# Attention and mixture of experts on one core: x of three batches written in rows of 2 KB, w2 loaded in runs of eight rows

## The chip, the cores and the metric

The kernel runs on one core of a Trainium2 chip. The metric is the device time of one execution in microseconds (us). A profile gives the span of one execution, which is some 1.5 us shorter than the time (201.9 of 203.35 us in the profiled run of before, 207.6 of 209.21 in that of after). Engines are called PE (matrix multiplications), DVE (vectors), ACT (exponentials and other functions), POOL (GpSimd: casts, and the issues of the weight loads among others) and SP (only issues transfers). A transfer is cut into packets (47,856 in the profile of before), which 16 DMA engines move.

The run list gives each run a state. On one core, a run is put down as slow when it takes over 1.5% longer than the fastest of the same kernel. This matters below, because the kernel before turns out to have two ways of running.

## The reference

```python
# attention: 4 batches, 8 heads, 768 positions, 64 wide
scores = scale * q @ k.T                  # causal; some heads see all the past,
a = softmax(where(mask, scores, -1e9))    # the others 4 sinks and a window of 64
x = (a @ v).transpose(0, 2, 1, 3).reshape(3072, 512)
# mixture of experts: 8 experts, 512 -> 1024 -> 512
do = x @ w_skip > 0                       # tokens that are computed
e, gate = argmax / softmax of x[do] @ w_gate
out = x
out[do] = x[do] + gate * (relu(x[do] @ w1[e]) @ w2[e])
```

## The kernel before

Attention runs over 16 pairs of heads, four pairs to a batch. The loads of q, k and v and the stores of x are issued by SP. POOL casts each v to 16 bits (the tile `va`), casts the result x, and issues the loads of the expert weights at six fixed pairs. So the weights of the first experts are loaded while attention still runs.

```python
def load_weight():                        # on GpSimd; half 0 is w1, half 1 is w2
    ...
        nc.gpsimd.dma_start(              # w1: 8 KB runs
            out=wts[e, 0]..., in_=w1r[e][:, q0 * w:q1 * w])
    ...
        nc.gpsimd.dma_start(              # w2: runs of WR = 4 rows
            out=wts[e, 1].rearrange("p (t r) d -> p t (r d)", r=WR)[:, q0:q1],
            in_=w2r[e][:, q0:q1])

def load_v(i):                            # ld_pool has two buffers
    vf = ld_pool.tile([P, 2, NQB, D], FP32, tag="vf", name="vf")
    for hi, hh in enumerate(hs):
        nc.sync.dma_start(out=vf[:, hi], in_=vv[b, :, hh])

# weigh(i, hi), after the product with v:
    if not last:
        ins = nc.gpsimd.tensor_copy(x16s[i], xh[:, :, h2:h2 + 2])
        if i in (0, 5, 10, 11, 12, 13):
            with tc.issue_after(ins.ins):
                load_weight()
    if i >= NPR - 2:                      # the last batch: a store for each pair
        ...
    elif i % 2 == 1:                      # the others: a store for two pairs,
        hc = (i // 2) % 2                 # half a row of x, 1 KB
        nc.sync.dma_start(
            out=Ov[b][:, :, hc * 4 * D:(hc + 1) * 4 * D],
            in_=xh.rearrange("p n h d -> p n (h d)"))

# the main loop
    cast_v(i)
    load_qk(i + 3)
    load_v(i + 2)
```

Pairs count from 0. Pairs 14 and 15 are the last two, and batch 2 consists of pairs 8 to 11. The store of x after pair 11 is issued near 92 us, and the v of pair 15 is loaded right behind it on the same queue.

The softmax here doesn't subtract the row's maximum and nothing guards it: scores larger than these inputs give would overflow.

Of the kernel before, what the change touches and what calls it, by code (L numbers as in the profile page):

```python
# [9 lines left out]
FP32 = mybir.dt.float32  # L10
FP16 = mybir.dt.float16
I32 = mybir.dt.int32
# [28 lines left out]
MASKED = 30000.0  # L41
WR = 4

# [216 lines left out]
def kernel(  # L260
# [27 lines left out]
    ones16 = const.tile([P, P], FP16, name="ones16")  # L288
    tmpi = const.tile([P, P], I32, name="tmpi")
    iota16 = const.tile([P, P], FP16, name="iota16")  # L290
# [3 lines left out]
    lim = const.tile([P, E], FP32, name="lim")  # L294
    pidi = const.tile([P, 1], I32, name="pidi")
    val = const.tile([P, N // P, 4], FP16, name="val")
    tabl = const.tile([1, H], FP32, name="tabl")
# [66 lines left out]
    wtile(E // 2, 0, wpool)  # L364
    xgs = [const.tile([P, DM], FP32, name=f"xg{t}") for t in range(NT)]


    w1r = moe_w1.rearrange("e (p s) f -> e p (s f)", p=P)
    w2r = moe_w2.rearrange("e (t p r) d -> e p t (r d)", p=P, r=WR)

# [3 lines left out]
    def load_weight(quarters=2):  # L374

        e, half, q0 = todo[0]
        q1 = q0 + quarters
        assert q1 <= 2
        del todo[:quarters]
        if half == 0:  # L380
            w = DS * F // 2
            nc.gpsimd.dma_start(
                out=wts[e, 0].rearrange("p s f -> p (s f)")[
                    :, q0 * w:q1 * w], in_=w1r[e][:, q0 * w:q1 * w])
        else:
            nc.gpsimd.dma_start(
                out=wts[e, 1].rearrange("p (t r) d -> p t (r d)", r=WR)[
                    :, q0:q1],
                in_=w2r[e][:, q0:q1])

# [19 lines left out]
    with tc.tile_pool(name="ac", bufs=1) as ac_pool, \  # L410
         tc.tile_pool(name="ld", bufs=2) as ld_pool, \
         tc.tile_pool(name="qk_in", bufs=2) as qk_in_pool, \
         tc.tile_pool(name="qt", bufs=2) as qt_pool, \
         tc.tile_pool(name="xsb", bufs=3) as x_pool, \
         tc.tile_pool(name="st_ps", bufs=2, space=bass.MemoryType.PSUM) as st_psum, \
# [193 lines left out]
        def weigh(i, hi):  # L609
# [15 lines left out]
            for n, (qb, c, vb) in enumerate(plan):  # L625
                nc.tensor.matmul(  # L626
                    opsa[:, qb, :], ats[i][:, b0 + c:b0 + c + P], vb,
                    start=(n == 0), stop=(n == len(plan) - 1))
            if i % 2 == 0 and hi == 0:
                xhs[i // 2] = x_pool.tile([P, NQB, 4, D], FP32, tag="xh",  # L630
                                          name="xh")
# [6 lines left out]
            if last:  # L638
                nc.vector.tensor_mul(x16s[i][:, :, hi], opsa[:, :, :D],
                                     rec.to_broadcast([P, NQB, D]))  # L640
            nc.vector.tensor_mul(xhs[i // 2][:, :, 2 * (i % 2) + hi, :],  # L641
                                 opsa[:, :, :D],
                                 rec.to_broadcast([P, NQB, D]))
            if hi == 0:
                return
            xh = xhs[i // 2]
            h2 = 2 * (i % 2)
            if not last:
# [4 lines left out]
            if i >= NPR - 2:  # L653
                nc.sync.dma_start(
                    out=Ov[b][:, :, hs[0] * D:(hs[1] + 1) * D].rearrange(
                        "p n (h d) -> p n h d", h=2),
                    in_=xh[:, :, h2:h2 + 2])
            elif i % 2 == 1:
                hc = (i // 2) % 2
                nc.sync.dma_start(  # L660
                    out=Ov[b][:, :, hc * 4 * D:(hc + 1) * 4 * D],
                    in_=xh.rearrange("p n h d -> p n (h d)"))

        def gate_transpose(i):
            xtp = tr_psum.tile([P, NQB, P], FP16, tag="tps", name="xtp")
            for n in range(NQB):
                nc.tensor.matmul(xtp[:, n],
                                 x16s[i][:, n].rearrange("p h d -> p (h d)"),
                                 C.ident,
                                 is_transpose=True, start=(n == 0),  # L670
                                 stop=(n == NQB - 1))
            xTg = gat_pool.tile([P, NQB, P], FP16, tag="gxT", name="gxT",
                                bufs=5)
            if i < NPR - 1:
                nc.scalar.activation(xTg, xtp, ACT.Copy)  # L675
            else:
                half = NQB // 2
                nc.vector.tensor_copy(xTg[:, :half], xtp[:, :half])
                nc.scalar.activation(xTg[:, half:], xtp[:, half:], ACT.Copy)
            xTs[i] = xTg  # L680
            if i == NPR - 2:
                nc.gpsimd.drain()
            if i == NPR - 1:

                nc.gpsimd.tensor_copy(mark, xTg[:, 0, :1])
                load_weight()
# [226 lines left out]
    with tc.tile_pool(name="moe_w", bufs=1) as mw_pool, \  # L913
# [50 lines left out]
        def first(e):  # L964
            ht = h_pool.tile([P, FS, CAP], FP16, tag="ht", name="ht")
            for f2 in range(FS // 2):
                hps = h_psum.tile([P, 2, CAP], FP32, tag="hps", name="hps")
                for fi in range(2):
                    fs = 2 * f2 + fi
                    for s in range(DS):  # L970
                        nc.tensor.matmul(  # L971
                            hps[:, fi, :],
                            wts[e, 0][:, s].rearrange(
                                "p (t c r) -> p t r c", c=P, r=WR)[
                                    :, fs // WR, fs % WR],
                            xTs[e][:, s, :], start=(s == 0),
                            stop=(s == DS - 1))
# [3 lines left out]
        def second(e):  # L981


            parts = ([(s2, 0, FS) for s2 in range(NSM)] if e < E - 1 else
                     [(s2, h, h + WR) for h in (0, WR) for s2 in range(NSM)])
            ypss = {}
# [95 lines left out]
```

## Time and profile before

| | before |
|---|---|
| time, median of 3 | 204.0 us (203.73, 204.0, 207.48) |
| span of the profiled run | 201.9 us |
| busy share of PE, ACT, POOL | 81%, 56%, 59% |
| cast of v of pairs 13, 14, 15 begins | 93.61, 108.94, 112.36 us |
| first matmul of the experts (hps) | 133.10 us |
| last matmul of the experts (yps) ends | 192.84 us |

The prediction shows the queues, the chain and the timelines. Three more views of before are wanted for comparison. The first is the stretch between attention and experts, by engine: the start and end in us, its length, then for each engine its busy time and number of instructions, then the granted PE clock, the DMA share and GB/s.

```profile
core 0: us, PE busy (x) PEld busy (x) DVE busy (x) ACT busy (x) POOL busy (x), PEclk, DMA share, GB/s
...
108.00:133.00 25.00, 17.76 (x179) 10.33 (x179) 13.93 (x46) 3.65 (x6) 12.85 (x20) 0.80 0.82 186
```

Seven of these 25 us have no PE work, and the clock was at 0.80 on average. The second view is the group of expert matmuls with the weight loads that feed them (busy us and mean ns behind the first bar):

```profile
L971 PE MATMUL hps<-xT,w 128*128 128x256 f16 x256 | 29.2, 273 | 1.2 <-DVE xT L961 1.2
L971 PEld LDWEIGHTS <-w 128*128 128x128 f16 x256 | 27.9, 113 | 2.8 <-issue 1.5
```

The third is PE's longest gap at the end of attention (start, length; in brackets the idle time before and what ended it):

```profile
109.82 1.26 PE L626 MATMUL opsa<-va,at 128*128 128x65 f16 x21 [4.03 <-POOL va L505]
```

### The profile page before, as it was taken

How to read it: one execution, taken by the hardware profiler on the slowest of the kernel's cores; microseconds unless marked ns; L12 is line 12 of the kernel's file. 1: busy time of each engine (PE TensorE's matmuls, PEld its weight loads, DVE VectorE, ACT ScalarE, POOL GpSimd, SP SyncE). 2: the span in 40 equal slices, each digit the busy share in tenths (PEclk: the TensorE clock that was granted, in tenths of full speed). 3: DMA queues.
4: the chain of work that ended last, by engine and by line, in shares of the span. 5: the costliest groups of instructions: out<-in, count | busy, mean ns of one | idle time of the engine just before them, and what ended most of it. 6: DMA issues, size and time to landing. Idle time of an engine off the chain costs nothing.

```text
span 201.9 us, 4741 instructions
## 1 busy us (share of the span) xinstructions
PE 163.2 (81%) x1896; PEld 119.3 (59%) x1896; DVE 109.5 (54%) x254; ACT 113.0 (56%) x164; POOL 119.3 (59%) x179
## 2 busy tenths in 40 slices
PE   0487999889888898888982757978999999999920
PEld 0366666676666676666852443378678678665700
DVE  5323666636899668997650678253444534534020
ACT  5998888897688977888891420035143144130400
POOL 7585499687387693788403901687858575133311
PEclk9999999999999999999998795999999999999985
DMA  5999699999899999999999899479999999999501
GB/s 173 295 345 287 169 174 238 316 327 318 236 245 201 301 343 296 342 266 214 215 275 232 204 234 174 103 181 246 232 239 233 239 245 233 235 245 248 165 14 63
DMA packets 47856, 47.12 MB, mean 233 GB/s; under 512 B 28484, under 2 KB 43588, under 8 KB 46802
## 3 DMA queue, kind: packets, MB, share of 16 engines
q0 software_dynamic: 6976, 21.56, 50.3%
q1 hardware_dynamic: 40850, 25.17, 44.3%
q8 instruction: 17, 0.28, 0.6%
q14 instruction: 13, 0.11, 0.2%
HBM read 56.64 MB, written 10.49 MB: 333 GB/s over the span
## 4 chain that ended last, share of the span: by engine, by line
ACT 27%; DMA 26%; PE 23%; issue 8%; DVE 7%; POOL 6%; POOLq 1%; SPq 0%; ACTq 0%; DVEq 0%
ACT at L606 15%; DMA out_dram<-xg,idx_s 14%; DMA vf<-in_v_dram 10%; PE pst L578 5%; ACT xg L507 4%; PE pst L588 4%; PE hps L971 4%; ACT qT L526 4%; ACT gxT L675 3%; PE opsa L626 3%; POOL out_dram L1001 2%; PE pst L595 2%; PE yps L991 2%; POOL xg L935 2%; DMA xg<-out_dram,idx_s 1%
## 5 line engine op out<-in xcount | busy, mean ns | idle before, releaser
L606 ACT ACTIVATE at<-pst 128x1024 f16<-128x1024 f32 (+2 forms) x76 | 61.3, 836 | 17.2 <-PE pst L600 13.3
L978 ACT ACTIVATE ht<-hps 128x512 f16<-128x512 f32 x32 | 19.1, 598 | 49.4 <-PE hps L971 49.4
L588 PE MATMUL pst<-qT,kz 128*128 128x128 f16 (+2 forms) x288 | 35.8, 242 | 2.5 <-ACT qT L526 2.1
L588 PEld LDWEIGHTS <-kz 128*128 128x128 f16 x288 | 24.1, 100 | 21.9 <-issue 12.8
L535 DVE COPY kz<-tps 64x768 f16<-64x768 f16 x28 | 26.6, 950 | 9.7 <-PE tps L518 9.3
L971 PE MATMUL hps<-xT,w 128*128 128x256 f16 x256 | 29.2, 273 | 1.2 <-DVE xT L961 1.2
L971 PEld LDWEIGHTS <-w 128*128 128x128 f16 x256 | 27.9, 113 | 2.8 <-issue 1.5
L578 PE MATMUL pst<-smask,ident 128*128 128x512 f16 (+1 forms) x60 | 22.3, 372 | 8.7 <-ACT at L606 8.7
L991 PE MATMUL yps<-w,ht 128*128 128x512 f16 x128 | 28.8, 379 | 0.0
L1001 POOL DMA_INDIRECT out_dram<-xg,idx_s x16 | 16.4, 1022 | 18.5 <-issue 8.5
L649 POOL CAST gx<-xh 128x768 f16<-128x768 f32 x15 | 12.4, 828 | 19.3 <-DVE xh L641 14.5
L999 DVE SCALAR_TENSOR_TENSOR xg<-yps,gsl,xg 128x512 f32<-128x512 f32 x16 | 12.0, 750 | 20.4 <-PE yps L991 20.3
L626 PE MATMUL opsa<-va,at 128*128 128x65 f16 x372 | 19.8, 196 | 4.0 <-POOL va L505 4.0
L935 POOL DMA_INDIRECT xg<-out_dram,idx_s x16 | 16.8, 1047 | 8.6 <-issue 4.3
L626 PEld LDWEIGHTS <-at 128*128 128x128 f16 x472 | 17.9, 99 | 5.4 <-issue 4.2
L505 POOL CAST va<-vf 128x768 f16<-128x768 f32 x16 | 14.0, 876 | 11.2 <-DMA vf<-in_v_dram 11.1
L637 DVE RECIPROCAL rec<-opsa 128x6 f32<-128x6 f32 x32 | 6.2, 194 | 26.3 <-PE opsa L626 25.9
L991 PEld LDWEIGHTS <-ht 128*128 128x128 f16 x128 | 12.3, 98 | 13.5
L641 DVE TENSOR_TENSOR xh<-opsa,rec 128x384 f32<-128x384 f32 x32 | 17.8, 556 | 1.3
L499 POOL CAST qin<-qf 128x768 f16<-128x768 f32 x16 | 13.1, 818 | 3.3 <-DMA qf<-in_q_dram 3.3
L499 POOL CAST kin<-kf 128x768 f16<-128x768 f32 x16 | 13.1, 822 | 1.0 <-DMA kf<-in_k_dram 0.8
L518 PE MATMUL tps<-ident,qin 128*128 128x128 f16 x96 | 8.7, 231 | 5.9 <-POOL qin L499 5.9
(117 smaller groups left out, 260.7 us busy)
## 6 DMA issues: line engine op xcount, KB each, us to landing
w<-in_moe_w_dram POOLq DMA_DIRECT2D x14, 1024.0 KB, 10.7
qf<-in_q_dram SPq DMA_DIRECT2D x16, 384.0 KB, 6.3
kf<-in_k_dram SPq DMA_DIRECT2D x16, 384.0 KB, 6.0
vf<-in_v_dram SPq DMA_DIRECT2D x32, 192.0 KB, 6.0
out_dram<-xh SPq DMA_DIRECT2D x7, 768.0 KB, 6.8
w<-in_moe_w_dram POOLq DMA_DIRECT2D x4, 512.0 KB, 12.4
out_dram<-xh SPq DMA_DIRECT2D x2, 384.0 KB, 5.2
xg<-out_dram,idx_s POOLq DMA_INDIRECT x16, 7.2
```

The source lines that it names most:

```text
L499: nc.gpsimd.tensor_copy(h16, qk32[name, i].rearrange("p h n d -> p n h d"))
L535: nc.vector.tensor_copy(to, ti[r])
L578: nc.tensor.matmul(pst[:, bank - c0:bank - c0 + mw], C.ident, rmask.unsqueeze(1).to_broadcast([P, mw // P, P]) if retr else smask[:, bank: ...
L588: nc.tensor.matmul(pst[:, cols], kz[:, j * P:(j + 1) * P], qT[i][:, qb * P:(qb + n) * P], start=mw <= 0, stop=mw <= 0 or last)
L606: nc.scalar.activation(ats[i][:, b0:b0 + cn], pst[:, :cn], ACT.Exp, scale=SCALE)
L626: nc.tensor.matmul(opsa[:, qb, :], ats[i][:, b0 + c:b0 + c + P], vb, start=(n == 0), stop=(n == len(plan) - 1))
L641: nc.vector.tensor_mul(xhs[i // 2][:, :, 2 * (i % 2) + hi, :], opsa[:, :, :D], rec.to_broadcast([P, NQB, D]))
L935: ins = nc.gpsimd.indirect_dma_start(out=xgs[t], out_offset=None, in_=out[:, :], in_offset=bass.IndirectOffsetOnAxis(ap=idx_s[:, t:t + 1], ...
L971: nc.tensor.matmul(hps[:, fi, :], wts[e, 0][:, s].rearrange("p (t c r) -> p t r c", c=P, r=WR)[:, fs // WR, fs % WR], xTs[e][:, s, :], sta ...
L978: nc.scalar.activation(ht[:, 2 * f2:2 * f2 + 2], hps, ACT.Relu)
L991: nc.tensor.matmul(ypss[s2], hts[e][:, fs, s2 * P:(s2 + 1) * P], wts[e, 1][:, fs, :], start=(fs == 0), stop=(fs == FS - 1))
L1001: ins = nc.gpsimd.indirect_dma_start(out=out[:, :], out_offset=bass.IndirectOffsetOnAxis(ap=idx_s[:, t:t + 1], axis=0), in_=xgs[t], in_off ...
```

## The change

Its intent is fewer and longer packets. x of the batches 0 to 2 is collected for all eight heads and stored once, in rows of 2 KB, where before each batch was stored in two halves with rows of 1 KB. w2 is laid out so that a partition reads eight consecutive rows in one piece, as it already read its rows of w1 in one piece. The larger x tiles are paid for with two x buffers instead of three, four transpose buffers instead of five, and a scratch tile that borrows another's place.

```diff
-WR = 4
+WR = 8
...
-    w2r = moe_w2.rearrange("e (t p r) d -> e p t (r d)", p=P, r=WR)
+    w2r = moe_w2.rearrange("e (p r) d -> e p (r d)", p=P)
...
-                out=wts[e, 1].rearrange("p (t r) d -> p t (r d)", r=WR)[
-                    :, q0:q1],
-                in_=w2r[e][:, q0:q1])
+                out=wts[e, 1].rearrange("p s d -> p (s d)")[
+                    :, q0 * w:q1 * w], in_=w2r[e][:, q0 * w:q1 * w])
...
-         tc.tile_pool(name="xsb", bufs=3) as x_pool, \
+         tc.tile_pool(name="xsb", bufs=2) as x_pool, \
...
-            elif i % 2 == 1:
-                hc = (i // 2) % 2
+            elif i % 4 == 3 or i == NPR - 3:
+                hc = hs[1] + 1
                 nc.sync.dma_start(
-                    out=Ov[b][:, :, hc * 4 * D:(hc + 1) * 4 * D],
-                    in_=xh.rearrange("p n h d -> p n (h d)"))
+                    out=Ov[b][:, :, :hc * D].rearrange(
+                        "p n (h d) -> p n h d", h=hc), in_=xh[:, :, :hc])
...
                             wts[e, 0][:, s].rearrange(
-                                "p (t c r) -> p t r c", c=P, r=WR)[
-                                    :, fs // WR, fs % WR],
+                                "p (c r) -> p r c", r=WR)[:, fs],
```

More of the change, by code (lines that the diff above doesn't have):

```diff
@@ L288 @@
     ones16 = const.tile([P, P], FP16, name="ones16")
-    tmpi = const.tile([P, P], I32, name="tmpi")
     iota16 = const.tile([P, P], FP16, name="iota16")
@@ L295 @@
     pidi = const.tile([P, 1], I32, name="pidi")
+    xgs = [const.tile([P, DM], FP32, name=f"xg{t}") for t in range(NT)]
+    tmpi = xgs[NT - 1][:, :P].bitcast(I32)
     val = const.tile([P, N // P, 4], FP16, name="val")
@@ L364 @@
     wtile(E // 2, 0, wpool)
-    xgs = [const.tile([P, DM], FP32, name=f"xg{t}") for t in range(NT)]
     w1r = moe_w1.rearrange("e (p s) f -> e p (s f)", p=P)
-    w2r = moe_w2.rearrange("e (t p r) d -> e p t (r d)", p=P, r=WR)
+    w2r = moe_w2.rearrange("e (p r) d -> e p (r d)", p=P)
     todo = [(e, half, qt) for e in range(E) for half in range(2)
@@ L385, in load_weight @@
         else:
+            w = FS * DM // 2
             nc.gpsimd.dma_start(
-                out=wts[e, 1].rearrange("p (t r) d -> p t (r d)", r=WR)[
-                    :, q0:q1],
-                in_=w2r[e][:, q0:q1])
+                out=wts[e, 1].rearrange("p s d -> p (s d)")[
+                    :, q0 * w:q1 * w], in_=w2r[e][:, q0 * w:q1 * w])
     SCALE = 1.0 / (D ** 0.5)
@@ L628, in weigh @@
                     start=(n == 0), stop=(n == len(plan) - 1))
-            if i % 2 == 0 and hi == 0:
-                xhs[i // 2] = x_pool.tile([P, NQB, 4, D], FP32, tag="xh",
+            if i % 4 == 0 and hi == 0:
+                xhs[i // 4] = x_pool.tile([P, NQB, H, D], FP32, tag="xh",
                                           name="xh")
@@ L640, in weigh @@
                                      rec.to_broadcast([P, NQB, D]))
-            nc.vector.tensor_mul(xhs[i // 2][:, :, 2 * (i % 2) + hi, :],
+            nc.vector.tensor_mul(xhs[i // 4][:, :, hs[hi], :],
                                  opsa[:, :, :D],
@@ L645, in weigh @@
                 return
-            xh = xhs[i // 2]
-            h2 = 2 * (i % 2)
+            xh = xhs[i // 4]
+            h2 = hs[0]
             if not last:
@@ L672, in gate_transpose @@
             xTg = gat_pool.tile([P, NQB, P], FP16, tag="gxT", name="gxT",
-                                bufs=5)
+                                bufs=4)
             if i < NPR - 1:
@@ L984, in second @@
             parts = ([(s2, 0, FS) for s2 in range(NSM)] if e < E - 1 else
-                     [(s2, h, h + WR) for h in (0, WR) for s2 in range(NSM)])
+                     [(s2, h, h + FS // 2) for h in (0, FS // 2)
+                      for s2 in range(NSM)])
             ypss = {}
```

## The prediction

> **What bounds the kernel now.** I read the page first (engines, queues, chain), then the timelines of PE, GpSimd and the SP queue around the one long wait of the chain, and last the trace's packet and landing records for that stretch.
>
> ```profile
> q0 software_dynamic: 6976, 21.56, 50.3%
> q1 hardware_dynamic: 40850, 25.17, 44.3%
> ACT 27%; DMA 26%; PE 23%; issue 8%; DVE 7%; POOL 6%; POOLq 1%; SPq 0%; ACTq 0%; DVEq 0%
> ```
>
> The packets of the two queues fill 94.6% of 16 engines' time, so there is hardly any free transfer time. Yet only 26% of the chain is DMA: most transfers are hidden. Three stages differ.
>
> Attention up to about 88 us: the chain is nearly all ACT (exponentials of 1.02 us). A transfer matters there only when a load comes too late.
>
> Experts, 133.1 to 192.8 us: PE has no gap, and every wait for a weight is absent. The timeline of PE ends:
>
> ```profile
> 178.82 7.07 PE L991 MATMUL yps<-w,ht 128*128 128x512 f16 x32
> 185.73 3.66 PE L971 MATMUL hps<-xT,w 128*128 128x256 f16 x32
> 189.22 3.62 PE L991 MATMUL yps<-w,ht 128*128 128x512 f16 x16
> ```
>
> The landing records show the last w1 complete at 184.3, 1.4 us before its use at 185.73. So experts are PE bound, with DMA only just keeping up: faster loads alone gain nothing here; the stage moves with its start.
>
> End of attention, 88 to 133 us: the chain has its one large transfer, the v load of head pair 14 (pairs count from 0):
>
> ```profile
> 88.72 0.37 SPq L492
> 89.13 19.65 DMA vf<-in_v_dram
> 108.96 0.82 POOL va L505
> 109.82 1.26 PE opsa L626 x21
> ```
>
> PE stood idle for 4.03 us before 109.82. The GpSimd and SP timelines say what this load competed with:
>
> ```profile
> 92.11 5.50 SPq L660 DMA_DIRECT2D out_dram<-xh  x1
> 97.79 10.47 SPq L492 DMA_DIRECT2D vf<-in_v_dram  x2
> 108.30 1.26 SPq L660 DMA_DIRECT2D out_dram<-xh  x1
> ```
>
> ```profile
> 108.94 0.83 POOL L505 CAST va<-vf 128x768 f16<-128x768 f32 x1 [10.09 <-DMA vf<-in_v_dram]
> ...
> 111.53 0.70 POOL L386 DMA_DIRECT2D w<-in_moe_w_dram  x1
> 112.36 1.16 POOL L505 CAST va<-vf 128x768 f16<-128x768 f32 x1
> ```
>
> By the packet records four weight loads (w1, w2, w1, w2) move at 88.7-97.1, 95.5-102.8, 102.4-108.7 and 113.0-119.7. While one runs, the SP queue gets next to nothing: v of pair 14 was issued at 88.72 and its first packet moved after 92.5; x stored at 115.29 moved from 119.0. The SP queue drains in the gaps between loads. One of the 16 engines lags about 1 us behind (an instruction fetch of 1.16 us at 96.0 may add to it), misses the gap at 95, and holds the last v packets until 108.8, when fifteen engines had delivered by 98.0.
>
> Behind that v stand, in order, x of batch 2 (issued 92.11) and v of pair 15 (97.79). The latter lands at 112.2 and is cast at 112.36: no slack, and the next weight load starts at 113.0.
>
> [...] where the SP packets were queued before the load: at 61-65 us there is about one v packet (256 B) to each w2 packet. Later issues got nothing until the load ended.
>
> [...] The change takes the step between w1 columns from 8 to 16 bytes[...]. The trace shows weight loads with the 8-byte step at 113 ns (L971) against 98 ns contiguous (L991); 16 bytes it doesn't show.
>
> [...] The trace has exactly 109 ns from start to start in L971. [...]
>
> **The change part by part.**
>
> *x rows.* Median packet times on the SP queue are 18, 27, 46 and 66 ns for 256, 512, 1024 and 1536 bytes, about 19 ns more per 512 bytes; I estimate 85 ns for 2048. One batch took 1536 x 46 / 16 = 4.42 us and will take 768 x 85 / 16 = 4.08: 0.34 us each, 1.0 us for three. Stores go from 7+2 to 4+2. But half of each batch moves to the later store. Batch 2's first half leaves 80.6 us and joins the store at 92.1, inside the crowded stretch. There the store keeps 768 packets, 48 per engine, each 39 ns longer: +1.9 us ahead of v of pair 15. The other two batches move from a partly idle stretch (56 us) or to 67.7, where the q loads have some 2 us before use.
>
> *w2.* Before, 256 packets of 4 KB (written size) at 324 ns: 256 x 324 / 16 = 5.18 us. After, 128 of 8 KB, as w1 has them, at 625 ns: 5.00 us. That is 0.18 us for each of six full loads, 1.1 us, of which 0.3-0.5 (fewer turns included) comes ahead of the critical v. The two halves of experts 3 and 7 stay in 8 KB runs of source. The three full loads among the experts only add slack.
>
> *w1 step.* If a weight load grows from 113 to, say, 140 ns, it still hides under the 109 ns matmul before it, since contiguous ones follow each other every 29 ns in L626. I take 0.
>
> *Buffers.* Two x buffers of a whole batch, four transposes and the borrowed scratch tile: each is free a batch or some steps before reuse. I take 0.
>
> *Sum on the path.* On the lagging engine: loads end at 107.2 instead of 107.5; then 48 v packets (0.9), 48 x packets (4.1 instead of 2.2), 96 v packets (1.8): 114.0 against 112.2-112.4. Alone that is +1.6 us. But the next w2 load, issued after the x16 copy that doesn't wait for this v, starts at about 112.7. The last 1.3 us of v would then wait until it ends at 117.7, and land at about 119: +7, less the 1.4 us of DVE work (Rall, oht) that now stands in the chain and would be done in the wait: +5.5 us.
>
> **The rivals.**
>
> 1. Pair 15's v is caught behind w2: 204 + 5.5 = 209.5. For: the 0.8 us between landing and the load's start, less than the added 1.6. Against: it needs the same lagging engine and order.
> 2. The lagging engine makes the first gap, so pair 14's v lands near 98 and PE's 4 us wait goes. For: fifteen did, and the backlog is 0.4 us smaller. But GpSimd, no longer held, issues w2 about 7 us earlier, before the doubled store has drained; pair 15's v then waits for its end, near 116.5. That gives +4.3 less 1.4: 207.
> 3. v is late by 1.6 us without being caught: 205.5.
> 4. Pure saving: 1-2 us of transfer time counts, and a shorter stall too: 200 to 203. For: both queues' 94.6%. Against: x and w2 savings lie mostly under ACT or PE, and experts can't shrink.
> 5. The 16-byte step slows PE: 256 matmuls, each ns past 109 costs 0.26 us. At 160 ns it would be +13. I give it 5%.
>
> **Range and chances.** I give rival 1 some 35%, 2 and 3 together 40%, 4 20%, 5 the rest. The middle is 206. The runs of before (203.73, 204.0, 207.48) show that this pattern tips by 3.5 us by itself, so the range is wide: 201 to 210.5. Faster than 199.9 needs more than the saved transfers: 13%. Slower than 208.1 is mainly rival 1 and a part of 5: 36%. Within 2%: 51%.
>
> **What would show it.** x packets of 2 KB near 85 ns and w2's of 8 KB near 625; L971 still 109 ns apart with weight loads over 113. PE gapless from the first hps to the end, so about 60 us there. The chain with one or two v loads between 88 and 120; the cast of va for pair 15 after 113.5 (116-120 in rivals 1 and 2), waiting on DMA. I am wrong if pair 15's v lands by 112 and the experts start before 132, or if hps is spaced wider than 109 ns.

## The result, and the profile after

| | before | after |
|---|---|---|
| time, median | 205.74 us (204.0, 207.48, 203.73, 207.85) | 209.55 us (209.21, 212.67, 209.0, 209.88) |
| span of the profiled run | 201.9 us | 207.6 us |
| cast of v, pairs 13, 14, 15 | 93.61, 108.94, 112.36 | 93.60, 99.00, 118.38 |
| load of expert 2's w2 issued | 111.53 | 106.37 |
| first hps | 133.10 | 138.71 |
| from first hps to the end | 68.8 us | 68.9 us |

The changed kernel is slower: the ratio of the fast runs is 1.027, with a 95% interval of 1.021 to 1.033. Ratios are the mean time of one kernel's fast runs over that of the other's fast runs of the same rounds, so they are not quite the ratio of the medians quoted. Here they rest on 209.21, 209.0 and 209.88 against 204.0 and 203.73. Both long runs of before fall outside as slow, which will need a second look. With all four runs of each kernel, the means are 210.2 and 205.8, or 2.1% apart.

The page after has these answers to the queue and chain lines of before:

```profile
q0 software_dynamic: 6208, 21.56, 48.6%
q1 hardware_dynamic: 38498, 25.17, 43.0%
...
DMA 26%; ACT 25%; PE 20%; POOL 10%; issue 10%; DVE 5%; POOLq 1%; ACTq 0%; SPq 0%; DVEq 0%
```

There are indeed fewer packets (44,736 in all against 47,856). The engines' time in them fell only a little: 48.6% of 207.6 us is 100.9 us against 101.6 before, and the other queue has 89.3 against 89.4. In the chain PE and ACT have given way to POOL and issue. The chain of waits tells where (start, length, piece):

```profile
93.60 0.84 POOL va L506
...
96.36 21.87 DMA vf<-in_v_dram
118.38 0.84 POOL va L506
...
138.71 3.65 PE hps L972 x32
```

The one long load in it is now that of pair 15, not of pair 14. The timelines of SP and POOL show its surroundings (start, length, queue or engine, line, operation, tiles; in brackets the idle time before and what ended it):

```profile
92.27 0.38 SPq L661 DMA_DIRECT2D out_dram<-xh  x1
94.46 13.08 SPq L493 DMA_DIRECT2D vf<-in_v_dram  x2
107.59 6.55 SPq L661 DMA_DIRECT2D out_dram<-xh  x1
```

```profile
99.00 0.84 POOL L506 CAST va<-vf 128x768 f16<-128x768 f32 x1
...
106.37 0.53 POOL L388 DMA_DIRECT2D w<-in_moe_w_dram  x1
118.38 0.83 POOL L506 CAST va<-vf 128x768 f16<-128x768 f32 x1 [11.48 <-DMA vf<-in_v_dram]
```

Before, POOL stood 10.09 us in front of pair 14's cast and only then issued the weight load, at 111.53. After, pair 14's v is there in time, POOL goes through, and the load is out at 106.37. Then POOL stands 11.48 us in front of pair 15's cast. PE follows it:

```profile
119.26 0.27 PE L627 MATMUL opsa<-va,at 128*128 128x65 f16 x2 [9.15 <-POOL va L506]
```

Its gap was 4.03 us before. The stretch table agrees: PE works 11.74 us where it worked 17.76, and at a lower granted clock, 0.66 where it was 0.80.

```profile
core 0: us, PE busy (x) PEld busy (x) DVE busy (x) ACT busy (x) POOL busy (x), PEclk, DMA share, GB/s
...
108.00:133.00 25.00, 11.74 (x136) 7.80 (x134) 11.24 (x42) 3.65 (x6) 4.77 (x11) 0.66 0.78 187
```

The expert matmuls themselves did not change:

```profile
L972 PE MATMUL hps<-xT,w 128*128 128x256 f16 x256 | 29.3, 273 | 1.2 <-issue 0.7
L972 PEld LDWEIGHTS <-w 128*128 128x128 f16 x256 | 28.4, 144 | 2.6 <-issue 1.5
```

A weight load takes 144 ns on average instead of 113, because of the wider step between columns: every run with w2's new layout has this step and near 144, every run with the old one near 113. It stays hidden: matmuls start 109 ns apart in both kernels, and the experts take as long as before.

The packet records show why pair 15's v came so late. The table counts packets that began in each microsecond, over all 16 engines, in the changed kernel:

```
us        w (8 KB)   x (2 KB)   v (256 B)
96           0         149        233      v of pair 14 ends
97           4         175          9
98          21          48          0      w2, expert 1, from 97.6
99          25          21          0
100         21          21          0
101         25          25          0
...
107         22          21          0      w1, expert 2
108         22          26          0
109          5         100         71
110         17          33        462      w2, expert 2, from 110.1
111         27           4         21
112         22           5         20
113         29           2         22
114         21           2         20
115         12           4        383
116          0           1        423
117          0           0        114      v of pair 15 landed at 118.2
```

In the rows from 99 to 101, and at 107 and 108, 21 to 26 packets of x began beside 21 to 25 weight packets; in those from 111 to 114, 20 to 22 packets of v began beside 21 to 29. So while these weight loads ran, about one packet of the SP queue began for each weight packet, with 2 KB as with 256 bytes; such a place between weight packets is called a turn below. For the 2 KB packets of x that is 42 KB or more in a microsecond. For the 1536 small packets of v it is some 5 KB: 20 to 22 packets, against 423 in the microsecond from 116 us, where no weight packet began. Without weight packets beside them they need some 1.8 us of engine time (an estimate: 96 packets for each engine at some 19 ns, between this trace's median of 18 and mean of 20.7). The only such stretch, between the weight loads near 109.5, went to what was left of x and to a third of v. The rest waited for the end of the next weight load, as this one was issued early enough to follow at once.

### The profile page after: what moved, and what is told of

Same layout as the page of the kernel before. It is cut to its first block, busy times and chain, and to the rows that moved or that the text cites. A ratio compares the mean times of both kernels' runs of the same rounds, so it can differ in the third digit from the quotient of the medians.

```text
span 207.6 us, 4736 instructions
## 1 busy us (share of the span) xinstructions
PE 162.3 (78%) x1896; PEld 119.7 (58%) x1896; DVE 110.5 (53%) x254; ACT 112.9 (54%) x164; POOL 118.0 (57%) x179
## 2 busy tenths in 40 slices
DMA packets 44736, 47.12 MB, mean 227 GB/s; under 512 B 28436, under 2 KB 38932, under 8 KB 42914
## 3 DMA queue, kind: packets, MB, share of 16 engines
q0 software_dynamic: 6208, 21.56, 48.6%
## 4 chain that ended last, share of the span: by engine, by line
DMA 26%; ACT 25%; PE 20%; POOL 10%; issue 10%; DVE 5%; POOLq 1%; ACTq 0%; SPq 0%; DVEq 0%
ACT at L607 15%; DMA out_dram<-xg,idx_s 14%; DMA vf<-in_v_dram 11%; PE pst L579 4%; ACT xg L508 4%; PE hps L972 4%; ACT qT L527 3%; PE pst L589 3%; POOL out_dram L1002 3%; ACT gxT L676 3%; PE opsa L627 2%; POOL xg L936 2%; PE pst L596 1%; DMA xg<-out_dram,idx_s 1%; PE xtp L668 1%
## 5 line engine op out<-in xcount | busy, mean ns | idle before, releaser
L978 ACT ACTIVATE ht<-hps 128x512 f16<-128x512 f32 x32 | 19.0, 597 | 49.5 <-PE hps L972 34.4
L972 PEld LDWEIGHTS <-w 128*128 128x128 f16 x256 | 28.4, 144 | 2.6 <-issue 1.5
L579 PE MATMUL pst<-smask,ident 128*128 128x512 f16 (+1 forms) x60 | 21.7, 361 | 9.3 <-ACT at L607 9.2
L1000 DVE SCALAR_TENSOR_TENSOR xg<-yps,gsl,xg 128x512 f32<-128x512 f32 x16 | 12.0, 751 | 20.3 <-PE yps L992 19.0
L676 ACT ACTIVATE gxT<-xtp 128x768 f16<-128x768 f16 x15 | 12.1, 807 | 11.9 <-PE xtp L668 11.9
```

Of the source, the lines that this page charges most:

```text
L579: nc.tensor.matmul(pst[:, bank - c0:bank - c0 + mw], C.ident, rmask.unsqueeze(1).to_broadcast([P, mw // P, P]) if retr else smask[:, bank: ...
L676: nc.scalar.activation(xTg, xtp, ACT.Copy)
L972: nc.tensor.matmul(hps[:, fi, :], wts[e, 0][:, s].rearrange("p (c r) -> p r c", r=WR)[:, fs], xTs[e][:, s, :], start=(s == 0), stop=(s == ...
L978: nc.scalar.activation(ht[:, 2 * f2:2 * f2 + 2], hps, ACT.Relu)
```

## The experiments

The theory (A) was that the whole loss comes from the store of batch 2: its double size stands in front of pair 15's v, and the early weight load then catches that v. The main rival (B) was that w2's longer packets starve the SP queue. Further rivals (other stores, buffers, the row size of 2 KB) are told where they are tested. All runs gave correct results. All had three rounds, in which the profiled first look is not part of the ratio. Runs on one chip share the runs of before. With so few rounds, the record's verdict by the 2% rule is "unclear" for every experiment that has one, except "same" for batch 2 in halves; so the readings below rest on the intervals and on the sequences in the traces. Quoted times are medians, with the profiled run's events beside them.

**Only the x part** (the changed kernel with w2 as before).

```diff
-WR = 8
+WR = 4
-    w2r = moe_w2.rearrange("e (p r) d -> e p (r d)", p=P)
+    w2r = moe_w2.rearrange("e (t p r) d -> e p t (r d)", p=P, r=WR)
...
```

> The changed kernel with w2 loaded as before (256 packets of 4 KB, 8-byte step between w1 columns); the x rows and the buffers stay changed. Theory A (the v load of pair 15 stands behind the doubled x store of batch 2 and is caught by three weight loads in a row): 207.5 to 209.5 us, v of pair 15 cast at 116 to 118.5, the first hps at 137 to 139. Theory B (w2's packets of 8 KB leave the SP queue half as many turns, and that starves v): 203 to 205 us, v of pair 15 cast by 113.

Measured: 210.1 us (209.73 to 210.45), ratio 1.029 (1.022 to 1.036). Pair 15's v was cast at 118.98 after a wait of 11.87, and hps began at 139.5. The x part alone carries the whole loss, so B falls as its cause.

**Only the w2 part** (the kernel before with the changed w2).

```diff
-WR = 4
+WR = 8
-    w2r = moe_w2.rearrange("e (t p r) d -> e p t (r d)", p=P, r=WR)
+    w2r = moe_w2.rearrange("e (p r) d -> e p (r d)", p=P)
...
```

> The kernel before with only w2 in runs of eight rows (and the 16-byte step between w1 columns); x stored as before. Theory A: 203 to 205 us in most runs, as before, with the same occasional slow run near 207.5; first hps near 133. Theory B: 207.5 to 209.5 us, v of pair 15 cast after 116. In both, hps matmuls 109 ns apart and weight loads of 143 to 144 ns.

Measured: 206.7 us (204.53 to 206.96), ratio 1.010 (0.999 to 1.020), which is unclear. The sequence is that of before: pair 14's v is cast at 109.33, pair 15's at 112.70. A cost of 1% is neither shown nor excluded by this run. In its trace 70.8 us pass from the first hps to the end, 2.1 more than in before. It is taken up again at the end.

**The weight load held back** (the changed kernel, the sixth weight load tied to pair 14's x instead of pair 13's).

```diff
-                if i in (0, 5, 10, 11, 12, 13):
+                if i in (0, 5, 10, 11, 12, 14):
```

> The changed kernel with one weight load (w2 of expert 2) issued one pair later, after the cast of pair 15's v, so that it cannot catch that v. Theory A: the weight queue is empty at about 109.5, x and v drain then, v of pair 15 is cast at 111 to 113.5, PE waits 2 to 3 us for it instead of 9.2, total 203 to 205 us. Theory C (the stretch is limited by the sum of transfers, so moving a load only moves the time): first hps still at 137 or later, 208 us or more.

Measured: 208.12 us (207.45 to 208.42), ratio 1.019 (1.012 to 1.026). This is a miss in time. The wait itself did what A says:

```profile
113.70 0.83 POOL L506 CAST va<-vf 128x768 f16<-128x768 f32 x1 [7.21 <-DMA vf<-in_v_dram]
...
117.20 0.53 POOL L388 DMA_DIRECT2D w<-in_moe_w_dram  x1
126.63 0.19 POOL L686 COPY mark<-gxT 128x1 f16<-128x1 f16 x1 [8.91 <-issue]
```

With the weight load out of the way, pair 15's v came 4.7 us earlier and PE's gap was 4.41 us. But the third line shows that POOL later stood 8.91 us in front of a copy. The page names no releaser; the trace has a drain of POOL there (L683 of the program, just ahead of the copy), which ran from 116.01 to 126.55, and the late weight load landed at 126.17. DVE then waited 2.71 us for POOL, and hps began at 138.03. The early weight load thus does catch v, and simply delaying it only moves the wait. As a test of the total this edit was confounded.

**Pair 15's v ahead of the store** (the changed kernel, the store of batch 2 issued after the load of pair 15's v).

```diff
+            elif i == 11:
+                held.append((Ov[b].rearrange("p n (h d) -> p n h d", h=H), xh))
...
             v32[i] = vf
+            if i == NPR - 1:
+                to, xh = held.pop()
+                with tc.issue_after(ins.ins):
+                    nc.sync.dma_start(out=to, in_=xh)
```

> The changed kernel with the x store of batch 2 issued after the v load of pair 15 instead of before it; same bytes, same rows. Theory A: v of pair 15 lands before 105, its cast waits for no DMA, PE has no wait over 3 us there, total 201 to 204.5 us. Theory C: the same bytes must still move, first hps at 136 or later, 207 us or more.

Measured: 205.89 us (201.63, 206.43, 205.36, 207.63), ratio 1.012 (1.002 to 1.021), which leaves out the profiled run. That is the one of 201.63:

```profile
88.94 6.79 SPq L494 DMA_DIRECT2D vf<-in_v_dram  x4
95.78 9.66 SPq L499 DMA_DIRECT2D out_dram<-xh  x1
```

```profile
106.44 0.53 POOL L388 DMA_DIRECT2D w<-in_moe_w_dram  x1
109.56 0.83 POOL L511 CAST va<-vf 128x768 f16<-128x768 f32 x1 [2.59 <-PE pst L606]
```

The weight load is as early as in the changed kernel, yet the cast no longer waits for a transfer; PE released it. PE's largest gap is 1.58 us. So an early weight load does no harm to a v that is queued ahead of x. The other three runs are 4 to 6 us longer. They were not traced, and what held them is open.

**Batch 2 alone back in halves** (the rest as in the changed kernel).

```diff
+            elif b == 2 and i % 2 == 1:
+                h0 = hs[1] - 3
+                nc.sync.dma_start(
+                    out=Ov[b][:, :, h0 * D:(h0 + 4) * D].rearrange(
+                        "p n (h d) -> p n h d", h=4), in_=xh[:, :, h0:h0 + 4])
             elif i % 4 == 3 or i == NPR - 3:
```

> The changed kernel with batch 2 alone stored in two halves again (1 KB rows, one half near 80.6 us, one near 92); batches 0 and 1 keep whole rows. Theory A (the doubled store of batch 2 ahead of pair 15's v is the loss): 203.5 to 207 us, first hps at 133 to 136, v of pair 15 cast at 112 to 115. Theory D (any of the other parts, buffers, w2, fewer stores, shifts v of pair 14 to the first gap and w2 then catches v of pair 15, whatever the store's size): 208 us or more, v of pair 15 cast after 116.

Measured: 204.75 us (203.23 to 205.53), ratio 1.000 (0.992 to 1.009). The timeline of POOL is that of before again:

```profile
109.07 0.83 POOL L506 CAST va<-vf 128x768 f16<-128x768 f32 x1 [10.07 <-DMA vf<-in_v_dram]
...
111.66 0.53 POOL L388 DMA_DIRECT2D w<-in_moe_w_dram  x1
112.49 1.16 POOL L506 CAST va<-vf 128x768 f16<-128x768 f32 x1 [0.30 <-DMA vf<-in_v_dram]
```

One store out of three undoes the loss. The merged stores of batches 0 and 1, the smaller number of buffers and the w2 part, which all stayed in, cost nothing that shows at 1%.

**Batch 2 alone in whole rows** (w2 as before, batches 0 and 1 in halves), the counterpart.

```diff
+            elif b < 2 and i % 2 == 1:
+                h0 = hs[1] - 3
+                nc.sync.dma_start(... 4 heads from h0 ...)
             elif i % 4 == 3 or i == NPR - 3:
```

> The changed kernel with w2 as before and batches 0 and 1 stored in halves as before; batch 2 alone is stored in whole rows. Theory A (the store of batch 2 in front of pair 15's v is the whole loss): like the changed kernel, 208.5 to 210.5 us; pair 14's v cast near 99, w2 of expert 2 issued near 106.3, pair 15's v cast 117 to 119.5 after a wait of 10 us or more on its load. Rival (the three merged stores are needed together, or the larger buffers): 203 to 206, pair 14's v cast near 109.

Measured: 209.52 us (208.59 to 209.83), with the sequence of the changed kernel:

```profile
99.13 0.83 POOL L506 CAST va<-vf 128x768 f16<-128x768 f32 x1
...
106.49 0.70 POOL L387 DMA_DIRECT2D w<-in_moe_w_dram  x1
118.67 0.83 POOL L506 CAST va<-vf 128x768 f16<-128x768 f32 x1 [11.48 <-DMA vf<-in_v_dram]
```

The store of batch 2 is thus needed for the loss, and enough for its sequence. The ratio, however, is only 1.010 (1.001 to 1.019), since before itself ran at a median of 207.76 us on this chip (205.73 to 209.55). That asks for a look at before.

**The kernel before, run as an experiment** (no edit).

> The kernel before itself, as a control: ratio 0.985 to 1.015, with single runs at both 203 to 205 and 207 to 208.5 us. If the profile falls in the longer kind, theory A expects v of pair 14 cast near 99 and v of pair 15 near 116, as in the changed kernel.

Measured: 207.32 us (208.15, 207.63, 203.62, 207.0). The profile fell in a long run of 208.15. It is put down as slow, so it is used here for its sequence and not for a ratio. Its chain of waits:

```profile
93.57 0.84 POOL va L505
...
96.44 20.63 DMA vf<-in_v_dram
117.21 0.84 POOL va L505
...
130.16 6.17 PE idle L776 x22
...
137.72 2.34 PE hps L971 x20
```

The kernel before runs in two ways. In the first, which the prediction saw, one DMA engine holds pair 14's v until 108.8; POOL is held too, the weight load goes out at 111.5, and pair 15's v slips in ahead of it. In the second, pair 14's v is in time (cast at 98.82), the weight load goes out at 106.18, and pair 15's v is cast at 117.21. The second sequence is that of the changed kernel. The times of before, over the 36 runs of it in this study's comparisons, can be split into two equal groups: 18 of 202.70 to 205.73 us and 18 of 206.35 to 211.66. The gap between them is small, and the shares differ: 6 of 7 short in one set of runs on chip 0, 1 of 7 on chip 8. Only one run of each group was traced, so that every long run has the second sequence is inferred. ("PE idle" in the chain is a name in the program for matmuls that only keep PE busy; they are no wait.)

The 16 runs of the four kernels that store all of batch 2 after pair 11 and hold nothing back (the changed one, the x part alone, batch 2 alone, and one that follows below) take 208.59 to 212.67 us. None is short. So the change seems to lose the short way of running, and in the traces its pair 15's v comes 1.2 to 1.8 us later than in before's long run.

**Both halves of batch 2 after pair 11** (w2 and batches 0 and 1 as before; place and bytes of the merged store, rows of 1 KB), first try.

```diff
+            elif i == 11:
+                for h0 in (0, 4):
+                    nc.sync.dma_start(... 4 heads from h0 ...)
             elif i % 4 == 3 or i == NPR - 3:
```

> As the run above, but batch 2 goes out in two stores of 1 KB rows, both issued after pair 11: the place and the bytes of the merged store without its row size. Theory A1 (the place counts: 768 packets of 1 KB more ahead of pair 15's v): as slow as the merged store or slower, 208.5 to 212, pair 15's v cast at 117 or later. Rival A2 (the row size counts: packets of 2 KB lose their turns to the weight loads more than packets of 1 KB): 203 to 206.5, pair 15's v cast by 113.5.

Measured: 208.72 us (205.55, 208.13, 210.08, 209.3), ratio 1.009 (0.999 to 1.019); pair 14's v at 110.89, pair 15's at 114.28. The SP timeline shows that this run did not test what it was meant to:

```profile
82.51 0.42 SPq L667 DMA_DIRECT2D out_dram<-xh  x1
```

The first half's data were ready, and its issue was placed at 82.51, near where before has it. In effect this is the kernel before with larger x tiles, and its runs spread like those of before on the same chip.

**The same, mended** (the first half's issue tied to the second half's).

```diff
+            elif i == 11:
+                ins = nc.sync.dma_start(... heads 4 to 7 ...)
+                with tc.issue_after(ins.ins):
+                    nc.sync.dma_start(... heads 0 to 3 ...)
```

> The run with both halves of batch 2 after pair 11, mended: there the first store was issued at 82.5 us all the same, as soon as its data were ready; here its issue is tied to the second store's, so that 1536 packets of 1 KB stand ahead of pair 15's v. Place (A1): 208.5 to 212 us in all runs within about 1.5 us of each other, pair 15's v cast at 117 or later, and no stretch without w packets between the last two weight loads. Row size (A2): a mix of runs as in the kernel before on the same chip, pair 15's v cast by 113.5 or, in the second pattern, at about 117, the mean within 1% of before's.

Measured: 210.98 us (209.43 to 212.0), ratio 1.038 (1.023 to 1.052) against before's fast runs; before's seven runs there were 202.7 to 211.66. SP and POOL:

```profile
92.32 0.57 SPq L666 DMA_DIRECT2D out_dram<-xh  x1
92.95 3.21 SPq L670 DMA_DIRECT2D out_dram<-xh  x1
96.27 12.75 SPq L493 DMA_DIRECT2D vf<-in_v_dram  x2
```

```profile
106.42 0.70 POOL L387 DMA_DIRECT2D w<-in_moe_w_dram  x1
118.90 0.83 POOL L506 CAST va<-vf 128x768 f16<-128x768 f32 x1 [11.78 <-DMA vf<-in_v_dram]
```

With rows of 1 KB the loss is as large as with 2 KB (the runs spread by 2.6 us rather than the 1.5 expected). The place and the bytes count; no effect of the row size shows.

**The first half after pair 15's v** (w2 as before; the store leaves 80 us as in the change, but nothing is added ahead of v).

```diff
+            elif i == 9:
+                held.append((... heads 0 to 3 ...))   # issued after v of pair 15
```

> As the first run, but batch 2 in halves: the first half is stored after the load of pair 15's v, the second half after pair 11 as before. So the early store leaves the stretch near 80 us as in the change, and nothing is added in front of pair 15's v. If the missing early store alone tips the kernel into the second pattern (pair 14's v near 99, w2 issued near 106): 206 to 208.5, pair 15's v cast near 117, like the long runs of the kernel before. If the doubled store is needed for it: pair 14's v cast near 109 or pair 15's v in time, 203 to 205.5.

Measured: 207.09 us (204.73, 208.68, 205.49, 208.79); no ratio was given. In the profiled run of 204.73:

```profile
106.62 0.70 POOL L387 DMA_DIRECT2D w<-in_moe_w_dram  x1
112.14 0.83 POOL L511 CAST va<-vf 128x768 f16<-128x768 f32 x1 [4.83 <-DMA vf<-in_v_dram]
```

The four runs fit no single expectation. This one fits the second in its time and in pair 15's v, though after a wait of 4.83 us; the runs of 208.68 and 208.79, which were not traced, are as long as the first said. Pair 14's v is in time here (cast at 99.25) and the weight load early, as in the second way, and yet pair 15's v arrives by 112. So the missing early store alone does not always make this v late. The packet records show the difference between these runs. The table counts the packets of x ahead of v that began before 98 us and from 98 to 109, the time by which half of the engines had delivered expert 2's w1, the first packet of expert 2's w2, and how many of the 1536 packets of pair 15's v had begun by 111.0:

```
run                        x <98   x 98-109   w1 done   w2 starts   v by 111
before, long run            377      377       108.4      109.1       1435
first half after v          588      179       109.2      109.6       1497
both halves, forced         617      443       109.6      110.7        456
batch 2 alone, whole rows   339      409       110.7      110.4        339
x part alone                325      411       110.5      110.3        338
changed kernel              327      290       109.9      110.1        533
```

In the first two runs all but a few of the 768 packets of x (1 KB each) are gone by 109, and v has the stretch around the change of weight loads to itself. In the long run of before, 13 of 16 engines deliver the second load of v by 110.3 and three only at 116.3 to 117.1. In the other four, more bytes of x move between the weight packets: 443 to 822 KB from 98 to 109 us, by the table's packets, against 377 and 179. Either x is still there when the stretch comes (the changed kernel, the forced halves), or x has been moved but has pushed w1's end to where w2 starts at once (the x part alone, batch 2 alone: w1 done at 110.5 and 110.7, w2's first packet at 110.3 and 110.4). Few of v's packets get through, and all 16 engines (15 in the x part alone) finish after 116. In the changed kernel w2's 8 KB packets also leave x fewer turns: 247 weight packets and 290 of x began from 98 to 109, against 340 and 377 in the long run of before.

**The kernel before with v first** (the store after pair 11 issued after the load of pair 15's v).

```diff
+            elif i == 11:
+                held.append((Ov[b][:, :, 4 * D:8 * D], ...))   # issued after v of pair 15
```

> The kernel before with the x store of pairs 10 and 11 issued after the v load of pair 15. Theory A: v of pair 15 no longer waits behind the store; if v of pair 14 is still held by one lagging engine, 202 to 204.5 us, otherwise 200 to 203; in the profile no cast waits for v of pair 15. Theory C (only the sum of transfers counts): 204 us as before, first hps at 133.

Measured: 200.77 us (200.7, 200.84, 206.9, 200.46), ratio 0.980 (0.972 to 0.989). Pair 15's v is cast at 109.98, released by PE, and hps begins at 130.68:

```profile
109.98 0.83 POOL L510 CAST va<-vf 128x768 f16<-128x768 f32 x1 [3.09 <-PE opsa L631]
```

It beats both kernels, with one long run of four that was not traced.

**The kernel before with three v buffers** (v loaded one pair earlier).

```diff
-            vf = ld_pool.tile([P, 2, NQB, D], FP32, tag="vf", name="vf")
+            vf = ld_pool.tile([P, 2, NQB, D], FP32, tag="vf", name="vf",
+                              bufs=3)
...
-                if i + 2 < NPR:
-                    load_v(i + 2)
+                if i == 0:
+                    load_v(2)
+                if i + 3 < NPR:
+                    load_v(i + 3)
```

> The kernel before with three buffers for v instead of two and each v load issued one pair earlier, so that the v of pairs 14 and 15 are queued ahead of the weight loads of 88 and 93 us. Theory A: no cast of v waits over 1 us after 85 us, PE's 4 us wait at 105.8 to 109.8 is gone, first hps at 127 to 130, total 198 to 202 us, with less scatter between runs. Theory C: the transfers queue elsewhere, first hps at 132 or later, 203 us or more.

Measured: 200.81 us (200.45 to 201.75), ratio 0.982 (0.975 to 0.989).

```profile
88.67 1.17 SPq L493 DMA_DIRECT2D vf<-in_v_dram  x2
92.07 13.68 SPq L661 DMA_DIRECT2D out_dram<-xh  x2
```

```profile
98.81 0.83 POOL L506 CAST va<-vf 128x768 f16<-128x768 f32 x1
...
106.17 0.70 POOL L386 DMA_DIRECT2D w<-in_moe_w_dram  x1
108.74 1.27 POOL L506 CAST va<-vf 128x768 f16<-128x768 f32 x1 [1.87 <-PE pst L601]
```

The v that is issued at 88.67 is that of pair 15 here, ahead of the store of x. No cast waits for a transfer, hps begins at 129.82, and none of the four runs is long. The two edits that put v ahead of x therefore work on the kernel before as well; what they take away is not the change's cost alone but a wait that both kernels have. The changed kernel with three v buffers was not run.

**The w2 part with three v buffers.**

```diff
-WR = 4
+WR = 8
-    w2r = moe_w2.rearrange("e (t p r) d -> e p t (r d)", p=P, r=WR)
+    w2r = moe_w2.rearrange("e (p r) d -> e p (r d)", p=P)
...
+                              bufs=3)               # vf, as in the run before
...
+                    load_v(i + 3)
```

> The kernel before with the w2 part of the change and three v buffers (v loaded one pair earlier). Theory A says that w2's longer packets take nothing from a v that was queued in time: 200 to 202 us, as with three v buffers alone (200.8), pair 15's v cast by 110. If w2's form costs about 1% by itself, as the run of w2 alone hinted (ratio 1.01): 202.3 to 204, with the two us at the end of the experts.

Measured: 202.42 us (199.6, 201.75, 203.09, 203.29), ratio 0.978 (0.969 to 0.987) against a before of 207.76 on that chip. Pair 15's v is cast at 108.34 and hps begins at 129.51, so w2's longer packets take nothing from a v that is queued in time. Its profiled run, 199.6, is the shortest of the study; its median lies between the two expectations, and it ran on another chip than the run before. From the first hps to the end its trace has 68.5 us, so the 2.1 us that the run of w2 alone lost there are no fixed cost of w2's form; the first half after v, with the old form, has 70.6. Whether the w2 part gains or costs something by itself stays open; the run of w2 alone leaves room for up to 2%. Of all versions, three v buffers on the kernel before has the steadiest gain.

## Why the prediction was right or wrong

**The time.** 206.0 was predicted, 209.55 measured, within the range of 201 to 210.5. What was held likeliest did not come: within 2% had 51%, slower by over 2% had 36%, and the ratio was 1.027.

**The step that failed.** It is the sum of rival 2: "That gives +4.3 less 1.4: 207." Its mechanism is what happened, step by step: pair 14's v landed early, PE's 4 us wait went, POOL issued w2 earlier (5.2 us, not about 7), and pair 15's v waited for that load's end. The mechanism was right; both terms of the sum were mis-sized.

- The 4.3 is "v then waits for its end, near 116.5" less the 112.2 of before. The w2 packets ended at 116.4, as said, but v landed at 118.2. The packets that it still had to move after that were left out, although the working itself gives them 1.8 us. The term is 6.0.
- The "less 1.4" supposed that work of DVE would be done during the wait. In all traced runs but the one with the held weight load, the first hps follows the cast of pair 15's v by 20.3 to 21.6 us, whatever the wait ahead of it:

| run | cast | hps | between |
|---|---|---|---|
| before | 112.36 | 133.10 | 20.74 |
| after | 118.38 | 138.71 | 20.33 |
| before, long run | 117.21 | 137.72 | 20.51 |
| batch 2 alone, whole rows | 118.67 | 139.24 | 20.57 |
| three v buffers | 108.74 | 129.82 | 21.08 |

The term is 0.4. With both, 204 + 6.0 - 0.4 is 209.6, against 209.0 to 209.88 in the fast runs. The traces show where the 1.4 stayed. The DVE work was indeed done earlier (110.85 to 111.69 in after), but it had run beside POOL's work: in both kernels POOL casts x after this v, PE's transposition of that x waits for it, and from the cast of v to that transposition pass 3.96 us in before and 3.60 in after. Another 0.34 us is gained up to the next transposition, and 0.29 lost from there to hps. PE's clock, 0.66 instead of 0.80 between 108 and 133 us, stands against the saving too; its share was not tested.

**The weights.** Rival 1, with its 35%, needed the lagging engine that rival 2 did without, and it did not occur in the trace of the changed kernel. That its 209.5 is almost the measured time is luck: it adds up another path. Rivals 2 and 3 had 40% together around 206; with rival 2 sized rightly, its part of that weight would have lain above 208.1. The working also built its main sum on the profiled run's lagging engine, and used the spread of 203.73 to 207.48 only to widen the range. That spread was the question: the long run of before is rival 2's sequence, already there in about half of the runs, as far as their times tell.

**Turns.** The working read that while a weight load runs "the SP queue gets next to nothing", and that later issues "got nothing until the load ended". That was too strong already for the trace it read: in the microsecond from 93 us, 20 packets of pair 14's v, issued at 88.72, began beside 23 of the first weight load. It also holds 35 to 49 packets of v beside 47 to 49 of w2 in each microsecond from 62 to 64. One packet for one is still too slow for 1536 small packets: at the 20 to 22 in a microsecond of the table above they would take some 70 us (an estimate).

**The x rows.** The estimate of 85 ns for a 2 KB packet met a median of 84, but the mean is 95.6, so that one batch took 768 x 95.6 / 16 = 4.59 us, not 4.08. The 1 KB packets of before have a mean of 49.5, not 46, which makes 1536 x 49.5 / 16 = 4.75 us. So a batch saved 0.16 us, not 0.34. The "+1.9 us ahead of v of pair 15" was the right place to look. That this store brings the loss is shown by batch 2 in halves (ratio 1.000), by batch 2 alone (209.52) and by the forced halves.

**The w2 rows.** 8 KB packets took 625 ns as predicted. That they would bring 0.3 to 0.5 us ahead of the critical v was wrong in the sequence that came: longer weight packets left fewer turns to x (247 weight packets from 98 to 109 us, against 340 in before's long run). As the x part alone lost just as much, it did not decide.

**The w1 step, the buffers, the experts.** All three held: weight loads of 144 ns ("over 113", and an assumed 140 in the working), matmuls 109 ns apart with loads of 113 ns and of 144, 68.9 us from the first hps to the end against 68.8, and no cost of fewer buffers with batch 2 in halves.

**Pure saving** (rival 4) fell. The reason given against it, that the transfers saved lie under other work, fits the traces: the stretch from the first hps to the end did not shrink.

**Left open:** what made three of four runs with v first on the changed kernel long, and one of four on the kernel before; what decides in a run of before whether one DMA engine holds pair 14's v.

## What to carry to other kernels

Before merging two stores into one with longer rows, see what is queued behind the later of the two: here the saved packets counted little, and the bytes moved ahead of it decided. Put the load with the nearest deadline ahead of stores that nobody waits for, by issue order or by one more buffer; on the kernel before this gave 2%, where longer rows lost more than 2%. If the few runs of a kernel differ by more than the change is worth, find out which sequences they show before predicting, because a change may do no more than fix one of them.

## What else the traces show

- In some stretches weight packets and packets of x shared the engines by packets and not by bytes. In before's long run 46, 45 and 43 packets of x of 1 KB moved beside 45, 43 and 45 weight packets of 4 KB in the three microseconds from 99 us; in the changed kernel 21, 21 and 25 of 2 KB moved beside 25, 21 and 25 of 8 KB. The load of 256-byte packets fared worst: 20 to 22 v packets beside 21 to 29 weight packets in each microsecond from 111 to 114. It is not so everywhere: in before 9 to 17 packets of x began beside 20 to 28 weight packets in each microsecond from 103 to 106; why was not shown.
- A weight load's end moved with what else was queued. From before's long run to the x part alone, the time by which half of the engines had delivered expert 2's w1 went from 108.4 to 110.5 us, and 338 instead of 1435 packets of v had begun by 111.
- The step from 8 to 16 bytes between w1 columns took a weight load of PE from 113 to 144 ns, and nothing was lost: the matmuls stayed 109 ns apart.
- Between 108 and 133 us PE's granted clock was at 0.5 for 3.41 us (from 109.92) and 6.83 us (from 120.16) in before, whose gap of PE ended at 109.82 after 4.03 us, and for 17.07 us (from 112.58) in after, whose gap ended at 119.26 after 9.15. With three v buffers PE's longest gap there was 1.53 us, and the clock was at half from 112.50 to 122.74 all the same. What the clock adds to the work behind the gap was not isolated.
- In ten of the fifteen traces, among them before and the one with the held weight load, the drain of POOL behind pair 14 ended 0.38 us after the last landing of the weight load issued before it (120.45 after 120.07, and 126.55 after 126.17). In after that load had landed at 116.87, before the drain began at 120.69.
- Two runs of before were traced, with two sequences of transfers: pair 15's v was cast at 112.36 in one and at 117.21 in the other. By their times the 36 runs divide into 18 of 202.70 to 205.73 us and 18 of 206.35 to 211.66.
